# Float64 weights to float32: four VectorE operations and one ScalarE pass for a pair, against two and two

## The chip, the cores and the metric

The kernel runs on one core of a Trainium2 chip. A core has a TensorE for matrix products (PE in the profile; PEld is its weight load), a VectorE (DVE), a ScalarE (ACT), a GpSimd (POOL) and a SyncE (SP), whose queue issues almost all DMA transfers here. The metric is the device time of one execution in microseconds (us). A profile shows one execution; its span runs from the first to the last instruction.

## The reference

The operator is a gated linear recurrence followed by a two-layer network. For each of 4 batches and 8 heads, over 768 tokens with a head width of 48, in float32:

```
f = sigmoid(f_logit)
state = f[t][:, None] * state + outer(k[t], v[t])
y[t] = q[t] @ state
```

The heads of a token are put side by side into a row x of 384, giving 3072 rows, and the network is

```
h = x @ w_in            # w_in 384 x 2048
g = h * sigmoid(1.702 * h)
out = g @ w_out         # w_out 2048 x 384, out 3072 x 384 float32
```

The two weights are float64. A core computes in float32, so the kernel loads their bits as pairs of 32-bit words and makes float32 numbers of them on the chip, once, at the beginning.

## The kernel before, in words

**Units.** The rows are worked on in 12 units of 256 tokens. For a unit the recurrence is written as products: scores in six levels (the matrix product `sc`, L425, between `X` and a copy `Kc` of half of it, made by ACT at L494), VectorE products that bring `X` to the next level (L519), masked copies of the scores into `A` (VectorE L485 and L466, ACT L475 for the last level), a transposed k (`tkn` on PE, L595, copied by ACT at L596 as `kn`), state updates (`st`, VectorE L667 and L668) and the outputs `y` (PE L534 and L689). ACT copies y into `yT` (L703), and SP moves it by DMA into `xT` (L753, L758), the input of the network. Raw q, k and f are turned by PE (`t`, L357) and copied by ACT (L362) in the first three units.

**Network.** A tile of h (L1100) is six matrix instructions over 256 rows of one unit, followed by an ACT pass that makes g of it (L1104); an o product (L1114) multiplies g with rows of w_out, and four products fill one sum, which ACT (L1164) or VectorE (L1166) takes out. h, o, the turned inputs and tkn share four PSUM banks in rotation. From unit 3 on the network uses sums of weights and inputs instead (L869, L1006), which is not touched here.

**Weights in pairs.** The weights come in 16 pairs, each 128 partitions by 768 numbers: two of w_in, two of w_out, four times over. `fetch_weights` issues the DMA of the next pair into `bits` (three buffers) from SP. Seen as words, `lo` and `hi` are every second word of bits. `begin_pair` issues the ACT pass and puts the VectorE operations on the list `todo`, with a None behind them. `convert` begins the next pair when todo is short enough, runs one operation from todo, and where the None comes up counts the pair as done and fetches the pair three further on.

**What ACT and VectorE do to a pair.** The Prelu pass reads hi as a float32 and scales it by 2^-112, which moves the exponent's bias; for a negative number the slope -2^32 sets the bit that becomes the sign. L230 shifts left by 3, which gives the float32 without the low word. L231 masks all but sign and exponent, L232 multiplies this with the low word and 2^-52, and L233 adds the two into w_in or w_out.

**The order.** TensorE's and GpSimd's order is as written in the program in the whole kernel; up to the end of unit 3's part the program's order holds for the other engines too. `opening` does unit 0 and converts pair 0. Then `merge(n, ...)` emits the parts of unit n (one for each level, and others) and between them products of the network from the list `fill`. A product is taken only if the pairs it reads are counted as done when the part starts (`ready`). After each part some calls of `convert` are made, a number worked out from `pieces` and `NOP` (L1239, L1240): 26 in unit 1, 24 in unit 2, 10 in unit 3, after 4 in the opening. Pairs 0, 1 and 2 are fetched in the opening, pair 3 only when unit 0's xT is on its way (L720).

Of the kernel before, what the change touches and what calls it, by code (L numbers as in the profile page):

```python
# [9 lines left out]
F32 = mybir.dt.float32  # L10
I32 = mybir.dt.int32
U32 = mybir.dt.uint32
AF = mybir.ActivationFunctionType
ALU = mybir.AluOpType
# [9 lines left out]
def kernel(  # L24
# [33 lines left out]
    nc = tc.nc  # L58
# [118 lines left out]
    pairs = []  # L177
# [9 lines left out]
            pairs.append((w_out[:, ff:ff + 2, :], [  # L187
                (lambda t: t[:], moe_w_out[ff * P:(ff + 2) * P, :].rearrange("(c p) f -> p c f", c=2))]))
    NPC = 2 * FG
    NOP = 4  # L190
    fetched, todo = {}, []
    state = {"fetch": 0, "begin": 0, "done": 0, "behind": 0}

    def fetch_weights(engine=nc.sync):
        n = state["fetch"]
        if n >= len(pairs):
            return
        state["fetch"] += 1
        if n == 3 and 0 not in xTs:
            state["fetch"] -= 1  # L200
            return
        dst, parts = pairs[n]
        if moe_w_in.dtype == F32:
            for part, src in parts:
                nc.sync.dma_start(out=part(dst), in_=src)
            return
        bits = wp.tile([P, 2 * DM * 2], I32, tag="bits", name=f"bits_{n}", bufs=PAIRS_AHEAD)
        by_dst = bits.rearrange("p (c f) -> p c f", c=dst.shape[1])
        for part, src in parts:
            engine.dma_start(out=part(by_dst), in_=src.bitcast(I32))  # L210
        fetched[n] = by_dst.rearrange("p c (f two) -> p c f two", two=2)

    def begin_pair(m):
        if m not in fetched:
            todo.append(None)
            return
        dst, bits = pairs[m][0], fetched.pop(m)
        ve, lo, hi = nc.vector, bits[..., 0], bits[..., 1]

        def tmp(tag, bufs):  # L220
            t = wp.tile([P, 2 * DM], F32, tag=tag, name=f"{tag}_{m}", bufs=bufs)
            return t.rearrange("p (c f) -> p c f", c=dst.shape[1])

        a, s = tmp("a", 2), tmp("s", 1)
        ai, si = a.bitcast(I32), s.bitcast(I32)
        nc.scalar.activation(a, hi.bitcast(F32), AF.Prelu, scale=2.0 ** -112, alpha=-(2.0 ** 32))
        todo.extend((
            lambda: ve.tensor_scalar(si, ai, 3, None, op0=ALU.logical_shift_left),  # L230
            lambda: ve.tensor_scalar(ai, si, -(1 << 23), None, op0=ALU.bitwise_and),  # L231
            lambda: ve.scalar_tensor_tensor(a, lo.bitcast(U32), 2.0 ** -52, a, op0=ALU.mult, op1=ALU.mult),  # L232
            lambda: ve.tensor_tensor(dst, a, s, ALU.add),  # L233
            None,
        ))

    def convert():

        if state["begin"] < len(pairs) and len(todo) <= NOP // 2:
            begin_pair(state["begin"])  # L240
            state["begin"] += 1
        if todo and todo[0]:
            todo.pop(0)()
        if todo and todo[0] is None:
            todo.pop(0)
            state["done"] += 2
            fetch_weights()
# [971 lines left out]
    def merge(n, fill, columns, share, pieces=0, hold=0, by=1.0, chores=[], per=3, deal=()):  # L1219
# [10 lines left out]
        for kind, fn in parts:  # L1230
# [7 lines left out]
            at_ops += converting.get(kind, 0)  # L1238
            most = pieces * NOP // 2  # L1239
            n_ops = min(int(most * at_ops / (by * total_ops)), most) - ops  # L1240
# [29 lines left out]
    def opening():  # L1270
# [18 lines left out]
        for l in range(NL):  # L1289
            chosen[:] = [2, 3][l % 2:][:1]  # L1290
            level(l)
            if l in (2, 3):
                next_f((0, 4)[l - 2:][:1])
            elif l < NL - 1:
                keep_up(1)
            if l == 1:
                begin_pair(0)
                state["begin"] = 1
# [9 lines left out]
        chosen[:] = [2, 3, 2, 3]  # L1308
        next_q()
        begin_pair(1)  # L1310
        state["begin"] = 2
        evacuate(NL - 1)
        units[0][1][-2][1]()
        next_gates()
        for _ in range(NOP):
            convert()
# [55 lines left out]
```

## Time and profile before

| | |
|---|---|
| median of 3 runs | 599.85 us (598.73 to 600.31) |
| profiled execution: span | 594.5 us (no other time of it is on the page) |
| PE busy | 574.9 us, 97% of the span |
| DVE busy | 429.5 us, 72% |
| ACT busy | 291.9 us, 49% |
| POOL busy | 138.4 us, 23% |
| Prelu pass, L228 | 16 times, 15.9 to 156.8 us |
| VectorE operations, L230 to L233 | 64 times, 29.8 to 171.7 us |

Busy time is the time in which an engine works on an instruction. The line of 40 digits for an engine cuts the span into 40 slices of 14.9 us; a digit is the busy share in tenths. A timeline row gives the start, the time from there to the end of a run of like instructions, the engine, line, operation, the written and read tiles, and in brackets how long the engine was idle before and what ended that. In a group row the figures behind the bar are busy time, the mean of one in ns, and the idle time before them.

### The profile page before, as it was taken

Reading aid. Unit: us, or ns where it says so; the run is one execution under the profiler, and the core shown is the slowest. Engines: PE = TensorE matmul, PEld = TensorE weight load, DVE = VectorE, ACT = ScalarE, POOL = GpSimd, SP = SyncE. Lnnn points to the kernel's source line nnn. Section 1 sums busy time; section 2 is a strip of 40 time slices with the busy share of each in tenths; the row PEclk is TensorE's granted clock in tenths of the full one; section 3 lists DMA queues with packets and bytes.
Section 4 is the critical chain, followed back from the end, with each engine's and each line's share of the span. In section 5 each row is a group of like instructions: output and inputs, shape, how many; then the busy total and the mean of one; then the engine's idle time right before and its main releaser. Section 6 shows DMA issues by size and latency. Waiting matters only on the chain.

```text
span 594.5 us, 18457 instructions
## 1 busy us (share of the span) xinstructions
PE 574.9 (97%) x7814; PEld 513.6 (86%) x7814; DVE 429.5 (72%) x696; ACT 291.9 (49%) x613; POOL 138.4 (23%) x214
## 2 busy tenths in 40 slices
PE   6879899999999999999999999999999999999997
PEld 6756776867768789999999999999999999999897
DVE  2898987964866858789778778786887786462284
ACT  4746643453334353474474474573663564452440
POOL 4031200230027216610610700800700602203000
PEclk9979999999999999999999999999999999999999
DMA  7947859840243552353552343553361211001000
GB/s 181 215 124 179 193 145 225 217 100 1 52 106 66 145 130 65 80 139 77 127 146 51 84 113 91 130 134 60 88 168 44 63 38 29 28 3 27 28 1 27
DMA packets 82834, 58.29 MB, mean 98 GB/s; under 512 B 33153, under 2 KB 74785, under 8 KB 82753
## 3 DMA queue, kind: packets, MB, share of 16 engines
q1 hardware_dynamic: 82416, 56.73, 38.9%
q8 instruction: 61, 1.00, 0.7%
q10 hardware_dynamic: 337, 0.39, 0.3%
q14 instruction: 20, 0.16, 0.1%
HBM read 43.98 MB, written 8.39 MB: 88 GB/s over the span
## 4 chain that ended last, share of the span: by engine, by line
PE 87%; DVE 7%; ACT 3%; issue 1%; DMA 1%; POOL 1%; SPq 0%; DVEq 0%; ACTq 0%
PE h L1006 17%; PE h L1100 13%; PE o_Y L869 11%; PE o L1114 10%; PE o_Z L869 8%; PE h_y L1006 6%; PE sc L425 6%; PE o_X L869 4%; PE o_W L869 4%; PE y L689 2%; PE t L357 2%; PE y L534 2%; PE sc L643 1%; DVE X L519 1%; ACT yT L703 1%
## 5 line engine op out<-in xcount | busy, mean ns | idle before, releaser
L1100 PE MATMUL h<-xT,w_in 128*128 128x256 f32 x384 | 89.6, 388 | 1.4 <-DMA xT<-yT 1.4
L523 DVE TENSOR_TENSOR X<-X,tot 128x1024 f32<-128x1024 f32 x45 | 57.0, 1266 | 39.8 <-PE sc L425 33.2
L1100 PEld LDWEIGHTS h<-xT,w_in 128*128 128x128 f32 x384 | 72.8, 193 | 13.8 <-DMA xT<-yT 2.4
L494 ACT COPY Kc<-X 128x512 f32<-128x512 f32 x72 | 48.4, 672 | 65.7 <-DVE X L523 51.5
L1114 PE MATMUL o<-w_out,g 128*128 128x384 f32 x192 | 65.5, 491 | 0.4 <-DVE w_out L233 0.4
L968 POOL TENSOR_TENSOR E<-xT 128x128 f32<-128x128 f32 (+1 forms) x32 | 17.9, 571 | 204.0 <-DMA xT<-yT 112.0
L1114 PEld LDWEIGHTS o<-w_out,g 128*128 128x128 f32 x192 | 35.4, 190 | 22.8 <-DVE w_out L233 1.0
L1006 PE MATMUL h<-E,w_in 128*128 128x128 f32 (+1 forms) x420 | 53.4, 275 | 0.0
L869 PE MATMUL o_Y<-T,S 128*128 128x192 f32 x288 | 50.6, 329 | 0.0
L1006 PEld LDWEIGHTS h<-E,w_in 128*128 128x128 f32 x420 | 50.1, 192 | 0.0
L1036 ACT ACTIVATE g<-g 128x512 f32<-128x512 f32 (+1 forms) x63 | 35.6, 584 | 26.0 <-DVE g L1034 25.3
L1104 ACT ACTIVATE g<-h 128x256 f32<-128x256 f32 x64 | 23.8, 382 | 49.0 <-PE h L1100 48.6
L869 PEld LDWEIGHTS o_Y<-T,S 128*128 128x128 f32 x288 | 46.8, 190 | 0.5
L1034 DVE TENSOR_TENSOR g<-g,h 128x512 f32<-128x512 f32 (+1 forms) x52 | 31.8, 632 | 14.3 <-PE h L1006 13.3
L485 DVE COPY_PREDICATED A<-masks,sc 128x256 f32<-128x256 uint32 (+1 forms) x98 | 42.0, 506 | 0.1
L703 ACT COPY yT<-y 48x256 f32<-48x256 f32 x88 | 32.2, 366 | 18.3 <-PE y L689 17.2
L372 POOL TENSOR_SCALAR F<-F 128x1024 f32<-128x1024 f32 x10 | 17.2, 1716 | 95.9 <-ACT F L375 84.3
L345 DVE STREAM_TRANSPOSE X<-raw 128x512 f32<-128x512 f32 x36 | 38.1, 1105 | 0.1
L425 PEld LDWEIGHTS sc<-X,Kc 48*64 48x64 f32 x1440 | 26.2, 136 | 11.1 <-ACT Kc L494 4.8
L425 PE MATMUL sc<-X,Kc 48*64 48x64 f32 x1440 | 31.0, 222 | 4.8 <-ACT Kc L494 1.9
L1034 DVE TENSOR_TENSOR g<-g,h_y 128x512 f32<-128x512 f32 (+1 forms) x26 | 16.5, 634 | 22.3 <-PE h_y L1006 21.4
L1025 ACT ACTIVATE g<-h 128x512 f32<-128x512 f32 (+1 forms) x46 | 26.1, 576 | 10.8 <-PE h L1006 10.6
(162 smaller groups left out, 1156.2 us busy)
## 6 DMA issues: line engine op xcount, KB each, us to landing
bits<-in_moe_w_out_dram SPq DMA_DIRECT2D x8, 768.0 KB, 7.2
raw<-in_f_logit_dram SPq DMA_DIRECT2D x48, 96.0 KB, 3.5
raw<-in_k_dram SPq DMA_DIRECT2D x48, 96.0 KB, 3.0
bits<-in_moe_w_in_dram SPq DMA_DIRECT2D x8, 576.0 KB
raw<-in_q_dram SPq DMA_DIRECT2D x44, 96.0 KB, 2.3
k_tok<-z SPq DMA_DIRECT2D x56, 64.0 KB, 1.8
kt<-k_tok SPq DMA_DIRECT2D x14, 256.0 KB, 2.8
out_dram<-osb SPq DMA_DIRECT2D x18, 192.0 KB, 2.7
```

The costliest lines, as they stand in the source:

```text
L345: nc.vector.transpose(view(out, at, [[HALF, NP], [step, R4], [R4 * step, 32]]), by_half[:, j, f].rearrange("p a (j d) -> p (a j) d", j=R4) ...
L425: nc.tensor.matmul(t["sc"][h][g * HS:(g + 1) * HS, a, s, :], lhsT=t["Kc", l][rows(h), x:x + HS], rhs=rhs(h, a, g), start=True, stop=True,)
L485: moved = nc.vector.copy_predicated(out=view(A, c * HALF + at, dims), mask=mask.bitcast(U32), data=got)
L494: nc.scalar.copy(c.rearrange("p (n two m) -> p n two m", two=2, m=m), view(X, KF * SLOT, [[2 * m, SLOT // (2 * m)], [(KR - KF) * SLOT + m, ...
L523: nc.vector.tensor_tensor(x, x, y, ALU.mult)
L703: nc.scalar.copy(view(yT[rows(h)], at, [[U, NP], [step, HS]]), py[columns(h, g), g, :, f, :])
L869: nc.tensor.matmul(t[name], lhsT=lhs(f), rhs=rhs(f), start=(new and i == 0), stop=(i == HF - 1), skip_group_check=True,)
L1006: nc.tensor.matmul(ph[:, t], lhsT=WA[a][:, f * P:(f + 1) * P], rhs=E[n][b], start=(root and t == 0), stop=not goes_on, skip_group_check=True,)
L1034: nc.vector.tensor_tensor(to, to, part, ALU.add if sign > 0 else ALU.subtract)
L1036: nc.scalar.activation(to, to, AF.Gelu_apprx_sigmoid)
L1100: nc.tensor.matmul(ph, lhsT=w_in[:, c, ff * P:(ff + 1) * P], rhs=xTs[n][:, c, :], start=(c == 0), stop=(c == NK - 1))
L1114: nc.tensor.matmul(t["po"], lhsT=g[ff // FG][:, ff % FG, tt * P:(tt + 1) * P], rhs=w_out[:, ff, :], start=(ff == ffs[0]), stop=(ff == ffs[ ...
```

## The change

The ACT pass of the high word is written back in place, and a second ACT pass turns the low word, scaled by 2^-29, into an integer `r` (its top bits, rounded, 0 to 8). VectorE then shifts the high word left by 3 as before and adds r to it as an integer; the sum's bits are the float32. The mask and the multiplication by the exponent are gone. NOP goes from 4 to 2, so the calls of `convert` are halved everywhere (13, 12 and 5, and 2 in the opening). A pair is begun when todo holds up to 3 entries, where it was 2: three entries are a whole pair that is still to be done.

```diff
-    NOP = 4
+    NOP = 2
...
-        a, s = tmp("a", 2), tmp("s", 1)
-        ai, si = a.bitcast(I32), s.bitcast(I32)
-        nc.scalar.activation(a, hi.bitcast(F32), AF.Prelu, scale=2.0 ** -112, alpha=-(2.0 ** 32))
+        r, s = tmp("a", 2).bitcast(I32), tmp("s", 1).bitcast(I32)
+        nc.scalar.activation(hi.bitcast(F32), hi.bitcast(F32), AF.Prelu, scale=2.0 ** -112, alpha=-(2.0 ** 32))
+        nc.scalar.activation(r, lo.bitcast(U32), AF.Copy, scale=2.0 ** -29)
         todo.extend((
-            lambda: ve.tensor_scalar(si, ai, 3, None, op0=ALU.logical_shift_left),
-            lambda: ve.tensor_scalar(ai, si, -(1 << 23), None, op0=ALU.bitwise_and),
-            lambda: ve.scalar_tensor_tensor(a, lo.bitcast(U32), 2.0 ** -52, a, op0=ALU.mult, op1=ALU.mult),
-            lambda: ve.tensor_tensor(dst, a, s, ALU.add),
+            lambda: ve.tensor_scalar(s, hi, 3, None, op0=ALU.logical_shift_left),
+            lambda: ve.tensor_tensor(dst.bitcast(I32), s, r, ALU.add),
             None,
         ))
...
-        if state["begin"] < len(pairs) and len(todo) <= NOP // 2:
+        if state["begin"] < len(pairs) and len(todo) <= NOP + 1:
```

## The prediction

> **What bounds the kernel now.** First the page: which engine is full, and where it is not.
>
> ```profile
> PE 574.9 (97%) x7814; PEld 513.6 (86%) x7814; DVE 429.5 (72%) x696; ACT 291.9 (49%) x613; POOL 138.4 (23%) x214
> ...
> PE   6879899999999999999999999999999999999997
> ...
> DVE  2898987964866858789778778786887786462284
> ...
> PEclk9979999999999999999999999999999999999999
> ```
>
> TensorE is busy 574.9 of 594.5 us. It is short of full only in the first 75 us (five slices) and at the end; the changed code runs from 15 to 172 us. So next the busy times by stretch (columns: stretch, length, then busy time of PE, PEld, DVE, ACT, POOL, the granted clock, DMA):
>
> ```profile
> 30.00:45.00 15.00, 10.70 (x197) 8.04 (x187) 13.70 (x19) 6.96 (x16) 4.40 (x6) 0.77 0.50 129
> 45.00:60.00 15.00, 13.00 (x198) 8.89 (x192) 13.28 (x24) 9.76 (x22) 1.51 (x1) 1.00 0.70 174
> 60.00:75.00 15.00, 13.79 (x314) 11.27 (x318) 14.24 (x24) 9.49 (x23) 3.98 (x6) 1.00 0.81 191
> 75.00:90.00 15.00, 15.00 (x141) 11.18 (x132) 12.29 (x24) 5.32 (x11) 0.77 (x1) 1.00 0.61 147
> 90.00:224.00 134.00, 134.00 (x1309) 100.76 (x1308) 94.20 (x137) 55.95 (x119) 28.88 (x28) 1.00 0.47 116
> ```
>
> From 75 to 224 us PE has no gap, so VectorE work removed there is worth nothing; conversions before 75 us, when DVE is busy 27.5 of 30 us and PE lacks 3.2 us, can be worth something. PE's timeline names what it waits for there:
>
> ```profile
> 54.04 2.20 PE L1114 MATMUL o<-w_out,g 128*128 128x384 f32 x6 [0.42 <-DVE w_out L233]
> 56.60 0.69 PE L425 MATMUL sc<-X,Kc 48*64 48x64 f32 x32 [0.36 <-ACT Kc L494]
> ...
> 60.38 0.63 PE L595 MATMUL tkn<-ident,X 128*128 128x128 f32 x4 [1.60 <-DVE X L519]
> ...
> 70.14 0.65 PE L689 MATMUL y<-X,st 48*48 48x64 f32 x28 [0.46 <-DVE st L668]
> 71.02 0.71 PE L425 MATMUL sc<-X,Kc 48*64 48x64 f32 x32 [0.22 <-DVE st L668]
> ```
>
> Together 3.06 us, all behind DVE (Kc at 56.60 is a copy of an X that DVE finished late). In the chain of waits, too, DVE's conversions alternate with its X products from 48 to 67 us. From 27 to 37 us the chain runs over ScalarE instead: copies of A, transposes, Kc, y, and at the end xT by DMA. ACT's timeline shows the two places where an added pass matters:
>
> ```profile
> 25.86 0.93 ACT L228 ACTIVATE a<-bits 128x768 f32<-128x768 f32 x1
> 27.18 1.51 ACT L475 COPY A<-sc 32x256 f32<-32x256 f32 x4 [0.39 <-DVE A L485]
> ...
> 93.25 0.62 ACT L494 COPY Kc<-X 128x512 f32<-128x512 f32 x1
> ...
> 100.58 0.90 ACT L228 ACTIVATE a<-bits 128x768 f32<-128x768 f32 x1 [0.37 <-DMA bits<-in_moe_w_out_dram]
> ```
>
> In the opening ACT has 0.39 us to spare before the A copies; and pair 11's weights land only at 100.5 us. Prices come from the groups (busy us, mean ns of one | idle before):
>
> ```profile
> L232 DVE SCALAR_TENSOR_TENSOR a<-bits,a 128x768 f32<-128x768 uint32 x16 | 15.4, 961 | 0.3
> ...
> L230 DVE TENSOR_SCALAR s<-a 128x768 int32<-128x768 int32 x16 | 10.1, 632 | 2.7 <-ACT a L228 1.8
> ...
> L233 DVE TENSOR_TENSOR w_out<-a,s 128x768 f32<-128x768 f32 x8 | 7.6, 955 | 0.1
> ...
> L618 ACT COPY kn<-kt 128x512 f32<-128x512 f32 x14 | 15.8, 1128 | 0.0
> L228 ACT ACTIVATE a<-bits 128x768 f32<-128x768 f32 x16 | 14.8, 925 | 1.0 <-DVE w_in L233 0.6 <-DMA bits<-in_moe_w_out_dram 0.4
> ```
>
> **The change part by part.** *DVE loses two operations a pair.* Undisturbed, the four take 0.56 + 0.56 + 0.96 + 0.96 = 3.04 us. The addition stays one two-input operation of 768 elements (0.96). The shift now reads every second word of bits instead of a dense tile: 0.56 if like L230, at most 0.96 if it falls to the rate of L232, which reads such a plane. I take 0.56 (same operation and type), so 1.52 us a pair are freed (1.12 at the other end), 24 us over 16 pairs (18); nearly all of it beside a full PE or beside a DVE that waits for PE.
>
> [...]
>
> *ACT gains a pass a pair.* The Copy reads a strided plane and writes densely, as L228 does: 0.92, of which 0.83 in a row of passes (two L362 in a row take 0.66 against 0.38 alone, so passes overlap by some 0.1). The Prelu now writes every second word. Below 0.92 nothing speaks for; above, L618 reads single words at a step of four and takes 1.13 for 512 elements where a plain Kc copy takes 0.62: 0.99 ns more an element, so at most 0.92 + 0.76 = 1.68. I take 0.92, since a step of two costs nothing on ACT's read side.
>
> *The calls.* Between the parts of a unit, convert() is called half as often, one DVE operation a call, so a pair ends after the same part as before and TensorE's order and its data gates are unchanged. In unit 1 the parts get 3,3,1,3,3,1,3,3,3,3 calls before, 1,2,0,2,1,1,1,2,1,2 after. But a pair now begins when the one before still has both operations left: its ACT passes are issued with the previous pair's shift, no longer with its addition. So ACT meets each load earlier. In turn bits is free for the next load after the shift (and the Copy, earlier), no longer after L232: SP, which stood 8.6 us before pair 6's load until 53.05, issues it at about 50.2, pair 7's at 53.8 instead of 58.06, and the raw k loads queued behind move too. The Copy also waits for the addition two pairs back (its r buffer); that is always earlier on DVE.
>
> *Opening.* Pair 0's Copy (+0.83) pushes the next Kc from 16.98 to 17.7; it is needed 0.56 us after its old end: 0.2 us late. Pair 1's Copy pushes A L475 past its spare 0.39: 0.83 - 0.39 = 0.44, inside which the 0.2 lies. So y, xT by DMA and the first h come 0.45 us later. The shorter DVE there gains nothing: the next products wait for ACT and xT.
>
> *Pair 3.* Its load lands 5.8 us after its issue at 37.62, at 43.4 (43.85 now). Its passes stand before the second g and the F of L362: g leaves at 45.6 instead of 43.7, the Kc after it at 47.2 instead of 46.16, needed by PE at 49.2. Hidden with 1.4 us left.
>
> *45 to 75 us.* PE's own work from sc at 45.95 (45.50 + 0.45) to the end of y L689 is 21.9 us, end to end 67.9, against 70.79 now. DVE keeps up: X at 56.6 instead of 59.55, tkn's input ready before PE asks at 58.2 (60.38 now), states no longer behind conversions. ACT is the next one late: A copies 56.7 to 58.2, pair 6's passes 1.76, kn 0.58, pair 7's passes 1.76, sum 0.48, kn 0.58, so the second kn ends at 63.2 where PE would want it at 62.4: 0.8 us lost. Then X L362 and Kc follow PE's t (67.6), yT ends 72.2 instead of 73.86, and sc, at 74.62 now, starts at 72.95. Gain at 75 us: 3.06 (waits gone) - 0.45 (opening) - 0.8 (kn) - 0.2 (new Kc waits) = 1.6 us. A shift at 0.96 delays DVE by 0.4 a pair and hits no wait in this list.
>
> *75 to 172 us.* PE is full, so ACT's lateness counts only where it uses up cover. Pair 11's passes move from the part after the second last products to the part before: ACT stands from 93.9 to 100.56 (old times) and leaves the Copy at 102.3; the sum copy L1164, now at 96.13, ends at 102.8. PE needs its bank at 104.49 (tkn): 1.7 us cover. With pairs 12 and 13 behind, the second kn ends at 110.8, wanted by PE at 111.58: 0.8 us cover. I cost both at nothing; if the load lands later than this, PE stalls by the excess. After 172 us nothing is changed, and a shift of PE is carried to the end.
>
> The sum against the profiled execution: span 594.5 - 1.6 = 592.9. The median is 599.85, so 5.35 us lie around the span (the page gives no other time for that execution); 592.9 + 5.35 gives 598.2.
>
> **The rivals.** *ACT becomes the bound (slower).* If writing every second word in place costs the 0.76 of the upper bound, the opening is late by 0.83 + 0.76 twice, less the covers, 2.2 instead of 0.45, and three passes before the second kn add 2.3: 1.6 gain becomes 2.4 loss and up to 3.2 with the waits behind them: 602 to 603. It decides from about 0.3 us more a pass. For it: ACT is busy 19 of 30 us there and three of its passes are in PE's way. Against: L228 reads at that step at full rate.
>
> *All of PE's gap is won (faster).* The kn wait is hidden and the added passes fall into ACT's gaps: 2.9 gained, 596.9. From 36 to 42 us PE is granted half the clock; the 12 first h products take some 2 us more there; if the full clock comes back sooner, 594.9. Against: the opening's chain gets no shorter.
>
> *Gain given back (no change).* The wait for pair 11, or shorter ones for pairs 4, 8 and 14, exceed the covers of 1.7 and 0.8: each us more is a us of PE. 2 us late gives 599.9, 4 us 601.
>
> [...]
>
> **How the numbers follow.** 0.3% is 1.8 us, about what can be told from no change. Forecast 0.46 (own range 596.9 to 599.1: faster 0.24, same 0.22); whole gap 0.16 (faster); ACT bound 0.24 (slower 0.22, same 0.02); given back 0.14 (same 0.10, slower 0.04). Faster 0.40, same 0.34, slower 0.26. The range 595.5 to 603 leaves out a part of the second and third cases, some 0.14.
>
> **What would show it.** Shift near 0.56 and DVE some 24 us less busy; ACT 15 us more, both passes 0.92; PE's waits at 54, 60 and 70 us gone, a wait for kn near 62; ACT idle some 6 us for bits before pair 11's pass; PE without gaps from 73 us on. A Prelu over 1.2 us, or PE gaps after 75 us, would make it wrong.

## The result, and the profile after

The changed kernel takes 606.18 us (median of 4 executions, 605.44 to 607.25) against 599.29 us (median of 4, 598.32 to 600.31) on the same chip: a ratio of 1.0122 with a 95% interval of 1.0099 to 1.0145. It is 6.9 us slower. The prediction was 598.2 us, in a range of 595.5 to 603.

The page of the changed kernel, to be read against the same lines of before:

```profile
PE 580.3 (96%) x7814; PEld 516.4 (85%) x7814; DVE 405.9 (67%) x664; ACT 303.7 (50%) x629; POOL 137.5 (23%) x214
...
PE   6869888999999999999999999999999999999997
...
PEclk9889998999999999999999999999999999999999
```

VectorE lost 23.6 us of work and ScalarE gained 11.8. TensorE has the same 7814 products but is 5.4 us longer busy with them, and two more of its 40 slices are below 9. The groups with the conversion's prices (busy us, mean ns of one | idle before):

```profile
L227 ACT ACTIVATE bits<-bits 128x768 f32<-128x768 f32 x16 | 14.7, 919 | 2.4 <-DMA bits<-in_moe_w_out_dram 1.9 <-DMA bits<-in_moe_w_in_dram 0.6
L228 ACT ACTIVATE a<-bits 128x768 int32<-128x768 uint32 x16 | 14.6, 912 | 0.1
L230 DVE TENSOR_SCALAR s<-bits 128x768 int32<-128x768 int32 x16 | 10.3, 646 | 1.4 <-ACT bits L227 0.8
L231 DVE CUSTOM_DVE_ANT_0 w_in<-s,a 128x1536 uint16<-128x1536 uint16 x8 | 8.0, 997 | 0.7 <-PE tkn L593 0.7
```

Undisturbed, every price is as forecast. But the last row holds something that the program's text does not show: the addition of 768 int32 numbers runs as a custom operation on 1536 16-bit halves. The answer for that line also names who waited for it. For the float32 addition of before (L233) that was:

```profile
who waited for it (us, times):
  PEld o L1114: 1.0, 2
  ACT a L228: 0.6, 1
  PE o L1114: 0.4, 1
```

No h product is among these. For the integer addition it is:

```profile
who waited for it (us, times):
  POOL N_c L928: 11.1, 1
  PEld h L1098: 7.4, 5
  PE h L1098: 5.1, 5
```

The stretches (length, then busy time of PE, PEld, DVE, ACT, POOL, the granted clock, DMA) and PE's timeline show where:

```profile
45.00:60.00 15.00, 15.00 (x222) 11.27 (x220) 9.72 (x19) 11.01 (x22) 1.50 (x1) 0.95 0.93 243
60.00:75.00 15.00, 12.51 (x294) 10.06 (x284) 8.16 (x17) 11.76 (x23) 3.24 (x6) 0.96 0.71 162
75.00:90.00 15.00, 12.81 (x103) 8.75 (x103) 9.78 (x19) 6.19 (x14) 0.00 (x0) 0.93 0.63 153
90.00:105.00 15.00, 13.29 (x108) 10.19 (x107) 4.94 (x11) 6.52 (x13) 0.00 (x0) 0.89 0.67 177
```

```profile
86.55 0.70 PE L1098 MATMUL h<-xT,w_in 128*128 128x256 f32 x2
89.43 6.70 PE L1098 MATMUL h<-xT,w_in 128*128 128x256 f32 x22 [2.19 <-DVE w_in L231]
...
96.69 0.70 PE L1098 MATMUL h<-xT,w_in 128*128 128x256 f32 x2
99.10 3.72 PE L1098 MATMUL h<-xT,w_in 128*128 128x256 f32 x16 [1.72 <-DVE w_in L231]
...
119.32 2.43 PE L1098 MATMUL h<-xT,w_in 128*128 128x256 f32 x10 [0.63 <-DVE w_in L231]
```

The stretch from 45 to 60 us is full, as hoped. The loss is after 75 us, where TensorE had no gap before. At each place two h instructions run, TensorE stands, and the rest follow. Before, the products at the first two places ran through:

```profile
82.54 5.45 PE L1100 MATMUL h<-xT,w_in 128*128 128x256 f32 x24
...
88.54 4.15 PE L1100 MATMUL h<-xT,w_in 128*128 128x256 f32 x18
```

VectorE's timeline of the changed kernel at the first place shows what ended the wait:

```profile
88.44 0.94 DVE L231 CUSTOM_DVE_ANT_0 w_in<-s,a 128x1536 uint16<-128x1536 uint16 x1
```

This is the ninth addition of the run, that of pair 8, and it ends at 89.38; the products go on at 89.43. A product is taken only if its pairs are counted as done when the part starts, so the products at the first two places read among pairs 0, 1, 4 and 5, whose last addition had ended at 62.4. They wait for weights that they do not read.

To see which stretch holds how much, the span is cut at three marks that every execution has: the first h product, the first h product after tkn, and y (64 instructions, L534 before, L532 after) of the next unit. The rows are worked out from PE's timelines; the three lengths are differences of starts, the last one up to the end of the span.

| execution | first h, us | to h after tkn | from there to y | from y to the end | span |
|---|---|---|---|---|---|
| before | 38.40 | 23.53 | 48.71 | 483.9 | 594.5 |
| changed | 42.06 | 20.92 | 58.70 | 483.8 | 605.5 |

The forecast gain is in the second column (2.6 us), a loss of 10.0 us in the third, and 3.7 us in the opening. The two spans differ by 11.0 us, the medians by 6.9; how much belongs to these two executions is shown at the end of the experiments.

### The profile page after: what moved, and what is told of

Read it like the earlier page. It is cut to its first block, busy times and chain, and to the rows that moved or that the text cites. A ratio compares the mean times of both kernels' runs of the same rounds, so it can differ in the third digit from the quotient of the medians.

```text
span 605.5 us, 18438 instructions
## 1 busy us (share of the span) xinstructions
PE 580.3 (96%) x7814; PEld 516.4 (85%) x7814; DVE 405.9 (67%) x664; ACT 303.7 (50%) x629; POOL 137.5 (23%) x214
## 4 chain that ended last, share of the span: by engine, by line
PE 82%; DVE 3%; ACT 0%; issue 0%; DVEq 0%; ACTq 0%
PE h L1004 17%; PE h L1098 12%; PE o_Y L867 12%; PE o_Z L867 8%; PE o L1112 8%; PE h_y L1004 6%; PE sc L423 5%; PE o_X L867 4%; PE o_W L867 4%; PE y L532 2%; PE sc L641 2%; PE y L687 2%; PE h_sc L1004 1%; DVE w_in L231 1%; PE tkn L593 0%; DVE X L521 0%
## 5 line engine op out<-in xcount | busy, mean ns | idle before, releaser
L1098 PE MATMUL h<-xT,w_in 128*128 128x256 f32 x384 | 93.6, 399 | 6.3 <-DVE w_in L231 5.1
L1098 PEld LDWEIGHTS h<-xT,w_in 128*128 128x128 f32 x384 | 74.7, 199 | 20.8 <-DVE w_in L231 7.4
L517 DVE TENSOR_TENSOR X<-X,tot 128x512 f32<-128x512 f32 x30 | 20.3, 689 | 25.9 <-PE sc L423 23.3
```

What stands on the lines that cost most here:

```text
L1098: nc.tensor.matmul(ph, lhsT=w_in[:, c, ff * P:(ff + 1) * P], rhs=xTs[n][:, c, :], start=(c == 0), stop=(c == NK - 1))
```

## The theories

**A, waits that are not needed.** w_in lies in three chunks of 2048 numbers a partition, and a pair writes 256 of each. Between the first and the last number of such a write lies all of the middle chunk. If the integer addition, put down as 16-bit halves, counts as a write of that whole stretch, the instructions of an h tile for the middle chunk (the third and fourth of its six) must wait for the newest addition into w_in, whichever pair it converts. In the built program they carry such waits: a tile of pair 0 waits for the addition of pair 8, a tile of pair 4 for that of pair 9, a tile of pair 9 for that of pair 12. The two instructions that run before each stop are those for the first chunk. Before, an h product waits for its own pair alone.

**B, ScalarE.** The second pass, and the earlier beginning of a pair, delay copies that TensorE waits for.

**C, the opening.** Two added passes before 40 us cost 3.5 us there, which are carried to the end, and a lower granted clock (0.986 against 0.994 in the two profiles) does the rest.

## The experiments

**Three additions, each into one chunk (against the changed kernel).**

```diff
-            lambda: ve.tensor_tensor(dst.bitcast(I32), s, r, ALU.add),
+            add,
...
+        def add():
+            if dst.shape[1] != NK:
+                ve.tensor_tensor(dst.bitcast(I32), s, r, ALU.add)
+                return
+            for c in range(NK):
+                ve.tensor_tensor(dst[:, c, :].bitcast(I32), s[:, c, :], r[:, c, :], ALU.add)
```

> The changed kernel with one edit: where a pair goes to w_in, its integer addition is issued as three, one per chunk of 256 floats, so that each writes one contiguous region. Bits and results are the same. Theory A (waits that are not needed: an integer addition into w_in counts as a write of all that lies between its first and last element, so h products of pairs converted long ago wait for the newest addition): TensorE's waits on this line between 85 and 120 us (2.19, 1.72 and 0.63 us in the changed kernel) go, and the time falls from 606.2 to 600 to 602 us, about 1.002 of the kernel before. Theory B (ScalarE's second pass delays what TensorE waits for) and theory C (3.5 us lost in the first 40 us are carried to the end and the rest is a colder clock): 605 to 607 us; three additions cost VectorE about 0.1 us a pair more.

Measured: 596.81 us (10 executions) against 598.75 of the kernel before (19), ratio 0.996, interval 0.9943 to 0.9976. So the edit takes back the whole loss and more, 1.6% of the time, and the form is faster than the kernel before. That is also below the 600 to 602 us that theory A gave: more than the length of the waits is gone. Nobody waited for the new additions into w_in; at the places where the changed kernel's TensorE stood, it runs through, at full clock:

```profile
83.30 5.45 PE L1105 MATMUL h<-xT,w_in 128*128 128x256 f32 x24
...
89.30 4.15 PE L1105 MATMUL h<-xT,w_in 128*128 128x256 f32 x18
```

```profile
75.00:90.00 15.00, 14.62 (x145) 10.91 (x146) 9.28 (x19) 7.56 (x15) 0.00 (x0) 1.00 0.58 143
90.00:105.00 15.00, 15.00 (x112) 9.78 (x112) 7.48 (x17) 4.30 (x9) 0.00 (x0) 1.00 0.77 195
```

The price is small: three additions take 1.08 us of VectorE's timeline where one takes 0.94.

**The kernel before with the integer addition alone.**

```diff
-            lambda: ve.tensor_scalar(ai, si, -(1 << 23), None, op0=ALU.bitwise_and),
+            lambda: ve.tensor_scalar(ai, si, 0, None, op0=ALU.bitwise_and),
...
-            lambda: ve.tensor_tensor(dst, a, s, ALU.add),
+            lambda: ve.tensor_tensor(dst.bitcast(I32), si, ai, ALU.add),
```

> The kernel before with its last conversion operation, the float32 addition, replaced by an int32 addition over the same tiles; the mask is set to zero so that the sum stays a valid number, which leaves the low word's part out of the weights. Number and length of operations on ScalarE and VectorE stay (four a pair on VectorE). Theory A: the same waits of h products on newer additions appear, and 599.3 becomes 602 to 606 us with gaps on TensorE between 75 and 120 us. Theories B and C: no difference, 598.5 to 600.5 us, since ScalarE has no second pass here.

Measured: 607.94 us (4 executions), ratio 1.017, interval 1.0119 to 1.0221, somewhat above the 602 to 606 of theory A. ScalarE and the number of VectorE operations are those of before, and the loss is all there, 9 us of it. The profiled execution is the slowest of the four (613.53 us, the others 607.20 to 608.01). Its waits:

```profile
PE h L1100 <- DVE w_in L233: 8.6, 6, 2.2
```

**The kernel before with ScalarE's second pass alone.**

```diff
+        nc.scalar.activation(hi, lo.bitcast(U32), AF.Copy, scale=2.0 ** -29)
```

> The kernel before with a second ScalarE pass a pair added (the changed kernel's Copy from the low words, its result written over the high words, which nothing reads again); VectorE keeps its four operations and its float32 addition. Theory A: within 1 us of the kernel before, 598.5 to 600.5 us. Theory B: 602 to 606 us. Theory C (the second pass in the first 40 us starts the loss): 601 to 603 us, and the first h product at 40 us or later where the kernel before has it at 38.4.

Measured: 598.33 us (10 executions), ratio 0.9993, interval 0.9977 to 1.0009: no difference. B falls as the cause of the loss, and C in its part on the added passes. (The earlier beginning of a pair, the other half of B, is not in this form; it is in the one with three additions, which loses nothing.) The first h product does start at 40.48, as C said; the last experiment shows why that is no evidence.

**Is it the int32 view, or the integer addition?** The next form keeps the changed kernel's two operations and one write in three chunks, and only replaces the addition.

```diff
-        nc.scalar.activation(r, lo.bitcast(U32), AF.Copy, scale=2.0 ** -29)
+        nc.scalar.activation(r, lo.bitcast(U32), AF.Copy, bias=-0.5, scale=2.0 ** -29)
...
-            lambda: ve.tensor_tensor(dst.bitcast(I32), s, r, ALU.add),
+            lambda: ve.tensor_tensor(dst.bitcast(I32), s, r, ALU.bitwise_or),
```

> The changed kernel with the same two operations on VectorE at the same places, but the last one a bitwise or of int32 words in place of the integer addition; for this the second ScalarE pass subtracts a half before it rounds, so that its integers stay within three bits (the weights are then truncated at the last bit, not rounded). One instruction a pair writes w_in, in three chunks, as the changed kernel's addition does. If the unneeded waits come from how the integer addition is put down (as 16-bit halves, whose strided destination counts as one whole stretch), the waits go: 596 to 598 us, as with three additions. If they come from viewing w_in as int32 at all, or from the weights being ready earlier, they stay: 604 to 607 us.

Measured: 598.36 us (10 executions), ratio 1.0006, interval 0.999 to 1.0021, just above the 596 to 598 expected. The waits are gone. The or of the same int32 views stays a plain operation on 32-bit words:

```profile
L231 DVE TENSOR_TENSOR w_in<-s,a x8: 937/964/1252, 32.1 to 132.7; 128x768 int32<-128x768 int32 x8
...
who waited for it (us, times):
  PEld o L1112: 0.4, 1
```

So it is the addition's form, with a destination in three pieces, that brings the waits; the view does not, nor do weights that are ready earlier. Why this form is slower than the three additions (the intervals 0.999 to 1.0021 and 0.9943 to 0.9976 do not meet) was not settled; in its profile TensorE loses 1.70 us to its own instruction issue before the next twelve h and takes 4.29 us for these, at a granted clock of 0.89 from 60 to 75 us; the other loses 1.35 and takes 2.86, at 1.00. That is one execution of each. The two later forms with an or come out like this one (0.9992 and 1.0001), the two later forms with three additions below it (0.9976 and 0.9955).

**Shift and or in one instruction (against the form with the or).**

```diff
-            lambda: ve.tensor_scalar(s, hi, 3, None, op0=ALU.logical_shift_left),
-            lambda: ve.tensor_tensor(dst.bitcast(I32), s, r, ALU.bitwise_or),
+            lambda: ve.scalar_tensor_tensor(dst.bitcast(I32), hi, 3, r, op0=ALU.logical_shift_left, op1=ALU.bitwise_or),
```

> The one before, with shift and or in a single VectorE instruction a pair. VectorE's busy time should fall by a further 6 to 9 us (16 shifts of 0.56 us). If VectorE still holds TensorE up anywhere before 75 us, 594 to 596 us; if what is left in that stretch is ScalarE, transfers and the opening, within 1 us of the two-operation form, 596 to 598 us.

Measured: 612.91 us, ratio 1.0261, interval 1.0236 to 1.0285. VectorE has 7.1 us less work than with two operations (399.0 against 406.1), as expected, and the form is the slowest of all: a pair now has one job, so each call of `convert` begins a pair. ScalarE's timeline:

```profile
43.49 0.91 ACT L227 ACTIVATE bits<-bits 128x768 f32<-128x768 f32 x1 [6.98 <-DMA bits<-in_moe_w_out_dram]
...
48.53 0.90 ACT L227 ACTIVATE bits<-bits 128x768 f32<-128x768 f32 x1 [2.81 <-DMA bits<-in_moe_w_in_dram]
```

It stands before loads that have not landed, with Kc, g and kn behind it, and TensorE waits for these:

```profile
PE sc L640 <- ACT kn L593: 5.7, 2, 4.1
PE sc L422 <- ACT Kc L491: 5.0, 2, 2.7
PE h L1097 <- ACT g L1101: 4.1, 1, 4.1
```

Neither expectation had it. The next run tests that reading with one empty job.

```diff
         todo.extend((
+            lambda: None,
             lambda: ve.scalar_tensor_tensor(dst.bitcast(I32), hi, 3, r, op0=ALU.logical_shift_left, op1=ALU.bitwise_or),
```

> The kernel with shift and or in one VectorE instruction (612.9 us), with one edit: an empty job ahead of it, so that a pair takes two conversion calls again, as in the changed kernel. If that kernel was slow because one call a pair begins the ScalarE passes of a pair before its load has landed (ScalarE stood 16.5 us for loads of bits there, 9.5 in the two-operation form, with copies of Kc and kn that TensorE needs queued behind), the time falls to 595 to 598 us. If the fused instruction itself, its wait on ScalarE or its read of the strided high words costs the time, it stays at 608 to 613 us.

Measured: 597.19 us (12 executions), ratio 0.9992, interval 0.9973 to 1.0011. The pace was the whole loss of 15 us. (The 9.5 us above are ScalarE's idle time for w_out in the form with the or; with w_in it is 10.1.) So theory B's mechanism exists, and costs that much where a pair takes one call, not two.

**The gain without the price.** The kernel before with two VectorE operations and one ScalarE pass; the low word is left out. NOP and the rule for beginning a pair are those of the changed kernel.

```diff
-            lambda: ve.tensor_scalar(ai, si, -(1 << 23), None, op0=ALU.bitwise_and),
-            lambda: ve.scalar_tensor_tensor(a, lo.bitcast(U32), 2.0 ** -52, a, op0=ALU.mult, op1=ALU.mult),
-            lambda: ve.tensor_tensor(dst, a, s, ALU.add),
+            lambda: ve.tensor_tensor(dst, s, s, ALU.max),
```

> The kernel before with only its VectorE operations cut to two a pair (the shift and a float32 operation that writes w_in; the low word is left out of the weights) and the begin rule of the changed kernel; ScalarE keeps one pass a pair. It is the gain without the price. If ScalarE's second pass costs nothing, the time equals that of the changed kernel with three additions, 596 to 597.5 us; if its share in the first 40 us is paid (first h product 1.9 us later than before), 594 to 595.5 us.

Measured: 594.73 us (5 executions), ratio 0.9943, interval 0.992 to 0.9966, that is 3.4 us less than before by the ratio. With its price (0.996) the change is worth 2.4; the price of 1 us is within the intervals. The profiles name a price: from the first h to y this form takes 70.39 us and the three additions 71.90, and the latter's waits for kn (0.73) and for the copy of a sum (0.52) are not in this one. The time falls into the range for a price paid in the first 40 us, but the first h product, at 39.55 against 40.30 in one execution each, does not show that.

**The second pass one call later (against the form with three additions).**

```diff
-        nc.scalar.activation(r, lo.bitcast(U32), AF.Copy, scale=2.0 ** -29)
...
+        def shift():
+            nc.scalar.activation(r, lo.bitcast(U32), AF.Copy, scale=2.0 ** -29)
+            ve.tensor_scalar(s, hi, 3, None, op0=ALU.logical_shift_left)
```

> The changed kernel with three additions per w_in pair, and the second ScalarE pass issued with the shift, one call later, so that the passes of pair 0 and 1 do not stand ahead of the copies of Kc and A in the opening. If those two passes cost the opening its time, the first h product starts before 39.5 us (40.3 with three additions alone, 38.4 before) and the time is 594.5 to 596 us; if the opening's loss has other causes (the clock, instruction issue, the load's landing), 596 to 598 us.

Measured: 596.86 us, ratio 0.9976, interval 0.9961 to 0.9991; first h product at 40.31. Nothing is won in the time; what the passes of pairs 0 and 1 cost the opening, one execution can't show (see the last experiment).

**The low word's pass on GpSimd (against the form with three additions).**

```diff
-        nc.scalar.activation(r, lo.bitcast(U32), AF.Copy, scale=2.0 ** -29)
+        nc.gpsimd.tensor_scalar(r, lo.bitcast(U32), 2.0 ** -29, None, op0=ALU.mult)
```

> The changed kernel with three additions per w_in pair, and the low word's pass on GpSimd (a multiplication written as integers) in place of ScalarE; ScalarE keeps one pass a pair. GpSimd is idle in 88% of the stretch from 35 to 120 us. If ScalarE's second pass is what separates 596.8 us from the 594.7 us of the form without it, 594 to 596 us. If GpSimd's pass is slow (2 us or more) or lengthens VectorE's operations beside it, so that additions come late, 597 to 602 us.

Measured: 595.51 us (12 executions), ratio 0.9955, interval 0.9936 to 0.9973: faster than the kernel before, and not to be told from the pass on ScalarE (0.996). GpSimd's pass is as slow as the second expectation asked, 2.2 us, and VectorE's shifts are longer on average (855 ns, 615 with the pass on ScalarE), but no wait of TensorE is put down to either.

**GpSimd's pass, and shift and or in one instruction (against the changed kernel).**

```diff
-        nc.scalar.activation(r, lo.bitcast(U32), AF.Copy, scale=2.0 ** -29)
+        nc.gpsimd.tensor_scalar(r, lo.bitcast(U32), 2.0 ** -29, -0.5, op0=ALU.mult, op1=ALU.add)
...
-            lambda: ve.tensor_scalar(s, hi, 3, None, op0=ALU.logical_shift_left),
-            lambda: ve.tensor_tensor(dst.bitcast(I32), s, r, ALU.add),
+            lambda: None,
+            lambda: ve.scalar_tensor_tensor(dst.bitcast(I32), hi, 3, r, op0=ALU.logical_shift_left, op1=ALU.bitwise_or),
```

> The two last forms together: the low word's pass on GpSimd, shift and or in one VectorE instruction, two calls a pair. VectorE's busy time should fall by 8 us or more against the form with GpSimd and three additions (595.5 us). If VectorE still sets anything that TensorE waits for, 593 to 595 us; if not, 595 to 597 us, the same. If the instruction's wait on GpSimd's pass (2.4 us each) holds VectorE's queue, with X and st behind it, 597 to 600 us.

Measured: 598.78 us (12 executions), ratio 1.0001, interval 0.9983 to 1.0018. VectorE has 9.9 us less work than in the form before and the time is 3 us longer, but not for the reason expected: VectorE did not wait for GpSimd's pass at all. In its profile TensorE stands 3.0 us in one place for nothing but its own issue, and 2.8 for xT. That execution took 600.76 us, near the upper end of the twelve (596.20 to 601.82); whether the stops are the form's or the execution's one profile can't tell.

**Both kernels a second time.** No edit.

> The kernel before, unchanged, profiled a second time. In its first profile the first h product starts at 38.40 us; in the ten forms profiled since it starts between 39.55 and 40.90 us, whether ScalarE has one pass or two a pair, and in the changed kernel at 42.06. If the opening differs from execution to execution by that much, it starts at 39.5 us or later here and the span is 596 us or more; if the short opening belongs to the kernel before, 38.2 to 38.8 us and a span near 594.5. From 61.9 to 110.6 us (first h product after tkn to y of the next unit) nothing should differ by over 0.5 us.

> The changed kernel, unchanged, profiled a second time. If the opening differs from execution to execution, the first h product starts between 39.5 and 41.5 us, not at 42.06. Theory A has TensorE's five waits for the integer addition into w_in here as well, some 5 us in all, and 56 to 60 us from the first h product after tkn to y of the next unit, where the kernel before takes 48.7.

Measured, one execution each: before 600.35 us, changed 600.29 us, beside 596.17 of the kernel before on that chip.

| execution | first h, us | to h after tkn | from there to y | from y to the end | span |
|---|---|---|---|---|---|
| before, first | 38.40 | 23.53 | 48.71 | 483.9 | 594.5 |
| before, second | 41.48 | 23.90 | 48.72 | 484.1 | 598.2 |
| changed, first | 42.06 | 20.92 | 58.70 | 483.8 | 605.5 |
| changed, second | 38.77 | 20.14 | 55.74 | 483.9 | 598.5 |
| three additions | 40.30 | 20.82 | 51.08 | 483.9 | 596.1 |
| before, second ACT pass | 40.48 | 23.52 | 48.77 | 483.8 | 596.6 |
| before, integer addition | 40.52 | 25.30 | 58.15 | 487.7 | 611.7 |

The last of these has one more such wait, of 2.03 us, after y.

The opening is a matter of the execution: 38.4 and 41.5 for one kernel, 42.1 and 38.8 for the other (earlier than the 39.5 expected). So the 3.7 us of the first comparison can't be put down to the kernel, and with them theory C loses its opening; its lower clock is looked at below. It is also the opening that lets the two second executions take the same time: it is 2.7 us shorter for the changed kernel, which loses 3.3 us from the first h to y. The second column differs by 0.4 and 0.8 us between executions of a kernel; in the third the kernel before repeats to 0.01 us, and the changed kernel takes 7 us more or 10. Its second profile has four of the five waits, with the same lengths (55.74 us in the third column, just under the 56 to 60 expected); only the first of 0.33 us, at 43.61, is missing:

```profile
PE h L1098 <- DVE w_in L231: 4.8, 4, 2.2
```

```profile
84.09 5.02 PE L1098 MATMUL h<-xT,w_in 128*128 128x256 f32 x22 [2.19 <-DVE w_in L231]
...
92.08 3.72 PE L1098 MATMUL h<-xT,w_in 128*128 128x256 f32 x16 [1.72 <-DVE w_in L231]
...
112.29 2.43 PE L1098 MATMUL h<-xT,w_in 128*128 128x256 f32 x10 [0.63 <-DVE w_in L231]
```

What follows the first of these waits differs: 22 instructions take 5.02 us here, and 6.70 in the first profile. The granted clock (third number from the end) of that stretch was 0.72 there and 1.00 here:

```profile
90.00:96.00 6.00, 6.00 (x21) 4.76 (x19) 0.63 (x2) 2.72 (x5) 0.00 (x0) 0.72 0.38 89
```

```profile
84.00:90.00 6.00, 5.91 (x56) 4.95 (x56) 1.40 (x4) 3.47 (x7) 0.00 (x0) 1.00 0.21 43
```

The loss in the third column thus splits. Against the three additions it is 55.74 - 51.08 = 4.66 us. The three waits are 2.19 + 1.72 + 0.63 = 4.54 us long, but they don't simply add up to it: the first two places take 2.46 and 1.98 us longer than there, waits and some 0.26 each of resuming, and the third only 0.10, since the three additions wait 0.52 for a copy of a sum at that place. The other 58.70 - 55.74 = 2.96 us of the first profile go with the lower clock: 6.70 - 5.02 = 1.68 in those 22 instructions, and 1.28 up to the sc behind the twelve h at 74.59, which followed a stop of 1.82 us at 73.3 and took 4.13 us instead of 2.86, at a granted clock of 0.78 from 75 to 80 us. So the size of the loss depends on the execution too. From the first h to y, this one takes 3.3 to 3.6 us more than the two of the kernel before, the first one 7.0 to 7.4. The four executions of the first comparison had a mean granted clock of 0.980 to 0.986, this one 0.994. The second profile has a stop of 2.19 us at the same place, and one of 1.46 where the first has 1.82, and was granted 1.00 behind both: so a stop of 2.19 us was followed by a lower clock in one execution of two, and what decides it was not shown.

## Why the prediction was wrong, and where it was right

**The step that failed is a half sentence under *The calls*:** "TensorE's order and its data gates are unchanged". The order is; the gates are not. I looked at which pairs a product reads and when they are converted, and took it that an operation with the same destination is waited for by the same products. The runs settle it: with the float32 addition of before, with the integer addition in three pieces, or with an or, there are no such waits; with the integer addition in one instruction, in either kernel, there are. In the changed kernel the three after 75 us are 4.54 us long, and up to 3 us more (2.96 in the first profile) go with the lower clock behind stops, 0.72 and 0.78 there. The forecast had the addition as "one two-input operation of 768 elements (0.96)", and 0.96 it took; its duration was the only thing that I asked of it.

**From 75 to 172 us**, the forecast costed the change at nothing, since PE is full there and only ScalarE's lateness could show. Its watch was on the wrong engine: the loss came over VectorE, which has time to spare there. "PE gaps after 75 us" was named as the sign that would make it wrong, and it is the sign that came.

**45 to 75 us.** All five waits of 3.06 us are gone, as worked out. The wait for kn, put at 0.8, is 0.67 and 0.73; the new Kc wait, put at 0.2, is 0.56 in the second profile and with three additions. Not foreseen was that TensorE, no longer held by VectorE's states, stops for its own issue before y at 69 to 73 us: 1.82, 1.46, and 1.35 with three additions, where before it waited 0.46 and 0.22 for st. In the second profile of the changed kernel, sc after the twelve h starts at 73.29 against 74.62 before; with the 0.37 by which its opening was later the gain at that point is 1.7 us, against 1.67 in the forecast (74.62 to 72.95). That agreement is luck: 0.68 of it is the first twelve h, before 45 us, which took 4.52 us from their start to the next t, and 5.20 before. From that t to sc the gain is 1.02 us, and 1.14 with three additions, where the forecast's terms without the opening give 3.06 - 0.8 - 0.2 = 2.06. The term that they lack is the stop for issue.

**The gain as a whole.** With three additions the kernel gains 0.4% (0.24 to 0.57), 2.4 us, and the forecast 592.9 / 594.5 is 0.27%, so the forecast's own range holds that time. Its mechanism is seen only in part. From the first h to y that profile takes 71.90 us, and the two of the kernel before 72.24 and 72.62, so 0.3 to 0.7 us of gain are seen there; the form with an or takes 71.94 and is no faster than before as a whole. Where the rest of the 2.4 us lies was not shown, and executions of one kernel differ by more in the opening.

**The opening**, put at 0.45 us, can't be read: executions of one kernel differ by 3 us there. The same holds for **the sum**: I took 5.35 us to lie around the span, as median less span. Every later execution has its span on record beside its time. In the kernel before 2.06 to 2.19 us lie around the span (600.35 - 598.2 is 2.15), in the changed kernel 1.75 to 1.84 (607.25 - 605.5 is 1.75). So the profile of before showed a fast execution, near 596.6 by an estimate from 594.5 and 2.1, with the short opening of 38.4 us, and the rest was no constant. The two errors stood in one number and cancelled, since I only used the difference.

**Pair 11.** ScalarE stands for its load as forecast ("some 6 us"): 7.97 us with three additions, up to 102.35. (In the changed kernel itself, whose TensorE was later by then, it stood only 1.9 us for loads of w_out in all.) The cover of 1.7 us, by which this was costed at nothing, did not quite do: TensorE lost 0.52.

```profile
106.37 2.86 PE L1105 MATMUL h<-xT,w_in 128*128 128x256 f32 x12 [0.52 <-ACT sum L1169]
```

**The prices.** Shift 0.56 us on every second word (median; the dense one of before, L230, 0.56 too), both passes 0.91 to 0.92, VectorE 23.6 us less (24 forecast). ScalarE gained 11.8 us of busy time, not 15; by group the Copy takes 14.6, and two passes in a row overlap (the first two begin 0.82 us apart, at 16.14 and 16.96, where the first takes 0.94). The Prelu's write to every second word costs nothing (919 ns, 925 before).

**The rivals.** *ACT becomes the bound* named the right sign with a wrong mechanism: with the second pass alone the time is 0.9993 of before. *All of PE's gap is won* (596.9 from 599.85) is nearest to the form with two operations and one pass, whose ratio of 0.9943 gives 596.4 on that scale. *Gain given back* named a load as the limit; 0.52 us of that was seen. Its two times, 599.9 for 2 us late and 601 for 4, do not follow from its own rule of a us for each us, by which they lie 2 us apart.

## What to carry to other kernels

When an operation is exchanged for another with the same operands, ask not only what it costs, but as what it is put down: its row in the profile (here 16-bit halves, a custom form) and who waits for it. The integer addition, with a destination in several pieces, came to hold readers of what lies between them; one write per contiguous piece took the waits away here for 0.14 us of VectorE a pair, and turned a kernel 1.2% slower than before into one 0.4% faster. And a second profile of the unchanged kernel is worth its run before a difference of 3 us at one place is explained.

## What the runs showed of the hardware that was not expected

- An int32 addition on VectorE appears as a custom operation on 16-bit halves, 128x1536, and still takes 0.95 us, as long as a float32 addition of 768 numbers (0.95 and 0.96 in the kernel before); an or of int32 takes 0.95 as a plain one.
- On GpSimd a multiplication of 768 uint32 numbers a partition, written as int32, took 2.2 us (median of 16, 2.18 to 3.60); the same with an addition behind the multiplication took 0.91 (0.88 to 1.49). The profile's spans on GpSimd are rough.
- TensorE stops for 0.2 to 3.0 us at a time for "issue" alone, in every profile and not always at the same places, between 24 and 75 us, and once at 119 (0.34). Before y at 69 to 73 us it does so in every form in which VectorE no longer holds it there, but for the one with the later second pass. What the issue lacks there was not tried.
